# One more written-out order for an attention and feed-forward kernel on a single core

## The chip, the core and the metric

The kernel runs on one core of a Trainium2 chip. A core has a matrix engine (PE, with its weight loads shown apart as PEld), a vector engine (DVE), a scalar engine (ACT), a general engine (POOL) and a queue engine (SP) that mostly starts transfers. Each engine works through its own list of instructions strictly in the order in which the program gives them, and waits at semaphores for what the others produce. The metric is the device time of one execution in microseconds (us), lower is better.

## The reference

The input is attention with a forget gate (batch 8, heads 8, sequence 576, head width 64), followed by a bilinear feed-forward layer over the 4608 tokens. Cut to what is computed:

```python
scores = q @ k.T / sqrt(64)                      # per batch and head, 576 x 576
cum    = cumsum(log(clip(f, 1e-4, 1)))           # along the sequence
scores = where(causal, -1e9, scores + cum[:, None] - cum[None, :])
attn   = exp(scores - rowmax); attn = attn / (rowsum(attn) + 1e-9)
x      = (attn @ v), heads side by side          # 4608 tokens x 512
out    = ((x @ w_a) * (x @ w_b)) @ w_out         # 512 -> 1536 -> 512
```

## The kernel before

**Attention.** Work is cut into pairs of heads: t = 0 to 31, four pairs for each batch b = t // 4. Two pairs form a half batch u = 0 to 15. Queries are taken in blocks of 128 rows, i = 0 to 4 (block 4 has 64 rows), and the blocks are put into four groups g: (1, 0), (2), (3), (4). For each half batch and group PE computes scores (`qk_group`, L390). In the first two batches the decay is added by PE itself, by two small matmuls, and DVE takes the row maximum (`do_max`, L484); later DVE adds the decay and takes the maximum in one instruction (`do_decay`, L508). Then ACT does the exponential with its sum (`do_exp`, L537 and L543), DVE the reciprocal (`do_recip`, L552), and POOL scales the probabilities (`do_norm`, L560). The probabilities are turned by PE in batch 0 (`pe_tr`, L584, copied out by a cast) and by a DMA transpose from the SP queue from batch 1 on (`do_tr`, L576): part A0 holds query blocks 0 and 1, A1 block 2, B blocks 3 and 4. PE multiplies them with v (`do_pv` L604 to L616, `do_pv4` L629), and a cast brings the result into the array xT. Casts on ACT have line L137, those on DVE and POOL L141, scaled ones on POOL L139.

**Inputs.** q, k and v of a batch are loaded in fp32 by the SP queue (L264, L280), cast to fp16 (by POOL, in batch 0 by ACT or POOL) and q and k are turned by DVE (`transpose_qk`, L294). The prefix sum of the gate runs at the start, on ACT (logarithm, L208) and DVE (L205 to L223), in two column parts, 0 to 255 and 256 to 575.

**Feed-forward.** Tokens are taken in chunks starting at t0 = 0, 256, 512 (256 tokens each), 768 (384), six of 512 tokens and a last one of 384. For each chunk twelve pairs of matmul groups (psa and psb, `ff_mm`, L877, four matmuls each), a cast of psa by ACT or DVE (`ff_copy`), a product by DVE (`ff_mul`, L888), then the output matmuls (pso, `ff_out`, L897), a copy (`ff_ocopy`) and a store. A chunk can begin when the attention of its tokens is in xT. The chunks of early batches are interleaved with the attention of later ones.

**Filler.** Forty filler groups (`filler`, L174), each of four matmuls of 128 columns on the identity matrix, occupy PE where nothing else stands; their result is not used. They need the identity, which POOL makes (`constants`).

**What sets the order.** Every step is created as an `Op` with a number (its place of creation), one or more engines that may do it, and its dependencies. The list `ORDER` gives the sequence in which the 2342 steps are emitted, and so the order on each engine; the letters of `CHOICE` give the engine of each step that could go to more than one. Both are written out by hand in the file; nothing is planned when the kernel is built. Rings of buffers (four for the PSUM tag ff, two for the scores sc, three for loads n32, two for cast inputs n16) are handed out in the same sequence, and a step that reuses a buffer waits for the users of its previous content. The field `size` of an `Op` is read by nothing in this file.

Numbers that the text below needs: 0 is the identity, 61 the clearing of padding (POOL). 45 and 60 are ACT's two table loads, 47 and 53 the two logarithms. 65 and 69 turn the first halves of k and q of batch 0 (DVE); 67 and 68 cast that half of q, 75 and 76 the other half; 49 and 50 make the rows of columns 0 to 255 of the prefix sum, 55, 56 and 57 those of columns 256 to 575 (DVE). 91 and 116 are the first score groups (g = 0) of half batches 0 and 1, 141 the second (g = 1) of half batch 0. 363 and 364 are the score groups g = 0 and g = 1 of half batch 3 (pairs 6 and 7), 367 and 395 their row maxima for block 1, 373 and 401 those for block 0, 368 is the first exponential of pair 6, 379 its maximum for block 2. 446 and 443 turn q and k of batch 2. 1680 and 1685 are the two output copies of chunk 0 and 1681 the store of the first. 467 is the first score group of half batch 4, 471 its first decay step, 426 and 435 the value products of blocks 0 and 1 of pairs 6 and 7. 345, 346 and 347 are the DMA transposes A0, A1, B of pair 4; 354, 355, 356 those of pair 5; 423, 424, 425 of pair 6; 432, 433, 434 of pair 7.

Of the kernel before, what the change touches and what calls it, by code (L numbers as in the profile page):

```python
# [37 lines left out]
def kernel(  # L38
# [13 lines left out]
    B, H, S, D = q.shape  # L52
# [7 lines left out]
    TW = S // NSLOT // 2  # L60
# [236 lines left out]
    def batch_inputs(b):  # L297
# [4 lines left out]
        for which, part, gm in items:  # L302
# [18 lines left out]
            ld = op("S", "ldqk", lambda _, which=which, hh=hh: load_qk(b, which, hh))  # L321
# [13 lines left out]
            tp = op("D", "tqk", lambda _, which=which, hh=hh: transpose_qk(b, which, hh), cas)  # L335
# [633 lines left out]
    for n in [256, 256, 256, 384] + [512] * 6 + [384]:  # L969
# [13 lines left out]
        215 81 216 202 203 276 204 7 201 180 207 208 281 285 181-183 1641 90 1642 441 187 317 289 188 189  # L983
        318 290 166 323 324 295 297 296 190 1645 1643 1644 319 325 217 218 1646 1647 165 1648 88 229 192 231
        459 291 221 223 191 230 257 224 258 209 232 255 222 279 184 256 280 286 235-237 444 238 329 205 186
# [5 lines left out]
        1682-1684 1680 316 364 340 249 1685 283 251 443 379 252 376 20 250 1687 404 380 1688 1691 398 381  # L991
        449 344 407 546 1689 1690 409 452 382 408 1693 372 1692 1695-1697 365 1694 347 348 371 464 349 357
# [6 lines left out]
        523 483 1737 1740-1742 492 493 488 489 509 494 524 510 477 516 539 525 526 1738 527 470 451 462 497  # L999
        498 1743 495 466 428-430 499 431 547 484 437 439 438 440 490 530 531 500 457 491 537 501 1745 1746  # L1000
# [4 lines left out]
        553 551 606 636 566 573 1791 574 557 558 575 576 607-609 653 1790 1793 1794 1792 637 559 578 577 579  # L1005
        555 610 611 580 552 1795 1798 1799 650 615-617 582-584 581 1796 560 639 548 612 642 556 620 622 627
        654 600 544 614 618 1800 1803 1804 1807 621 585 613 587 619 629 623 624 586 626 1805 625 630 1801
        588-590 1806 591 593 592 628 1808 1811 657 1809 1813 1810 1812 669 1815 1817 702 703 739 704 651
        1816 643 1814 709 670 705 1819 1820 638 710 655 1818 711 1823 676 1821 1825 671 1822 640 712-714
# [119 lines left out]
```

## Time and profile before

| what | value |
|---|---|
| median of 3 runs | 405.43 us (403.7 to 407.23) |
| the profiled execution, whole | 402.69 us |
| its span, first to last instruction | 400.9 us |
| granted PE clock, mean | 0.985 of full |
| PE busy | 378.9 us (95%) |
| DVE, ACT, POOL busy | 315.5, 250.6, 262.8 us |
| transfers, mean | 201 GB/s |

The profiled execution took 1.8 us more than its span; that is what lies before the first and after the last instruction. A table by stretch of time gives the busy time of each engine in it, the granted PE clock as a share of full speed, and the busy share of the 16 DMA engines (above 1 where packets overlap). A row of the timeline begins with its start in us from the beginning of the span and its length; in square brackets stands how long the engine sat idle before it and what ended that idle time. SPq is the issuing of transfers by the SP queue.

### The profile page before, as it was taken

How to read it: one execution, taken by the hardware profiler on the slowest of the kernel's cores; microseconds unless marked ns; L12 is line 12 of the kernel's file. 1: busy time of each engine (PE TensorE's matmuls, PEld its weight loads, DVE VectorE, ACT ScalarE, POOL GpSimd, SP SyncE). 2: the span in 40 equal slices, each digit the busy share in tenths (PEclk: the TensorE clock that was granted, in tenths of full speed). 3: DMA queues.
4: the chain of work that ended last, by engine and by line, in shares of the span. 5: the costliest groups of instructions: out<-in, count | busy, mean ns of one | idle time of the engine just before them, and what ended most of it. 6: DMA issues, size and time to landing. Idle time of an engine off the chain costs nothing.

```text
span 400.9 us, 10798 instructions
## 1 busy us (share of the span) xinstructions
PE 378.9 (95%) x3856; PEld 209.3 (52%) x3856; DVE 315.5 (79%) x958; ACT 250.6 (63%) x756; POOL 262.8 (66%) x438
## 2 busy tenths in 40 slices
PE   5679799989999999999999999999999999999996
PEld 5557575765846544444545454544454444444553
DVE  5879997979998988989899789899959893373450
ACT  2678895768768777758785777675868673310111
POOL 4988899787967796979696948697858753000000
PEclk9869999999999999999999999999999999999999
DMA  7999999999999999999899998999997827101102
GB/s 245 261 217 224 253 284 224 233 209 225 208 281 224 267 199 305 202 310 191 270 217 286 238 301 168 242 242 243 255 199 192 151 68 177 54 0 53 55 2 78
DMA packets 149466, 80.71 MB, mean 201 GB/s; under 512 B 130660, under 2 KB 133476, under 8 KB 149412
## 3 DMA queue, kind: packets, MB, share of 16 engines
q1 hardware_dynamic: 145492, 75.02, 79.1%
q0 software_dynamic: 3696, 4.72, 7.0%
q8 instruction: 30, 0.49, 0.5%
q10 hardware_dynamic: 224, 0.28, 0.2%
q14 instruction: 24, 0.20, 0.1%
HBM read 52.20 MB, written 9.58 MB: 154 GB/s over the span
## 4 chain that ended last, share of the span: by engine, by line
PE 69%; DMA 8%; DVE 8%; POOL 5%; ACT 4%; issue 4%; SPq 0%; POOLq 0%; ACTq 0%; DVEq 0%
PE psb L877 20%; PE psa L877 20%; PE pso L897 16%; PE sc L390 7%; DVE st L484 3%; PE pv L604 2%; DMA PTB<-PB 2%; POOL PA L560 2%; DMA spread<-cum_d 2%; DMA k<-in_k_dram 2%; PE idle L174 1%; DVE ht L888 1%; DVE S L508 1%; DMA out_dram<-osb 1%; DMA xT<-PA 1%
## 5 line engine op out<-in xcount | busy, mean ns | idle before, releaser
L877 PE MATMUL psb<-xT,wb 128*128 128x512 f16 (+2 forms) x528 | 115.2, 341 | 2.4 <-DVE a L141 1.3
L877 PE MATMUL psa<-xT,wa 128*128 128x512 f16 (+2 forms) x528 | 115.2, 341 | 0.5 <-ACT osb L137 0.2
L508 DVE CUSTOM_DVE_ANT_0 S<-sc,spread 128x128 f32<-128x128 f32 (+3 forms) x192 | 104.3, 567 | 7.8 <-PE sc L390 6.7
L560 POOL TENSOR_SCALAR PA<-PA,st 128x128 f16<-128x128 f16 (+2 forms) x180 | 84.4, 482 | 33.8 <-DVE st L552 19.8
L897 PE MATMUL pso<-wout,ht 128*128 128x512 f16 (+1 forms) x444 | 98.4, 374 | 0.0
L888 DVE TENSOR_TENSOR ht<-psb,a 128x512 f16<-128x512 f32 (+2 forms) x132 | 76.7, 588 | 14.1 <-PE psb L877 10.1
L543 ACT ACTIVATE PA<-S,st 128x256 f16<-128x256 f32 (+2 forms) x144 | 71.9, 501 | 22.9 <-DVE st L508 21.4
L877 PEld LDWEIGHTS <-wb 128*128 128x128 f16 x528 | 49.8, 98 | 45.7 <-issue 6.8
L877 PEld LDWEIGHTS <-wa 128*128 128x128 f16 x528 | 50.4, 98 | 42.7 <-issue 2.0
L560 POOL TENSOR_SCALAR PB<-PB,st 128x512 f16<-128x512 f16 (+1 forms) x90 | 62.8, 712 | 10.6 <-DVE st L552 5.9
L897 PEld LDWEIGHTS <-ht 128*128 128x128 f16 x444 | 41.8, 98 | 48.1 <-issue 2.8
L137 ACT CAST a<-psa 128x512 f16<-128x512 f32 (+2 forms) x85 | 42.7, 511 | 34.8 <-PE psa L877 33.4
L390 PE MATMUL sc<-kT,qT 32*128 32x128 f16 (+5 forms) x960 | 41.3, 272 | 6.8 <-DVE qT L294 4.6
L543 ACT ACTIVATE PB<-S,st 128x512 f16<-128x512 f32 x48 | 34.3, 716 | 8.1 <-DVE st L508 7.4
L484 DVE TENSOR_REDUCE st<-sc 128x1 f32<-128x576 f32 (+8 forms) x48 | 31.4, 693 | 6.8 <-PE sc L390 5.2
L141 DVE CAST a<-psa 128x512 f16<-128x512 f32 (+2 forms) x47 | 26.2, 558 | 11.3 <-PE psa L877 10.8
L390 PEld LDWEIGHTS <-qT 32*128 32x128 f16 (+1 forms) x960 | 19.0, 96 | 28.8 <-issue 12.3
L552 DVE RECIPROCAL st<-st 128x2 f32<-128x2 f32 x128 | 18.6, 157 | 11.5 <-ACT PB L543 6.1
L537 ACT ACTIVATE PB<-S,st 128x576 f16<-128x576 f32 x24 | 18.6, 775 | 13.9 <-DVE st L508 5.0
L543 ACT ACTIVATION_READ_ACCUMULATOR PA<-S,st 128x1 f32 x144 | 27.2, 189 | 0.0
L137 ACT COPY osb<-pso 128x512 f32<-128x512 f32 (+1 forms) x26 | 14.4, 563 | 20.3 <-PE pso L897 18.6
L141 POOL CAST k<-k 128x1152 f16<-128x1152 f32 (+2 forms) x16 | 22.1, 1384 | 5.0 <-DMA k<-in_k_dram 5.0
(87 smaller groups left out, 449.8 us busy)
## 6 DMA issues: line engine op xcount, KB each, us to landing
spread<-cum_d SPq DMA_DIRECT2D x24, 576.0 KB, 5.9
out_dram<-osb SPq DMA_DIRECT2D x35, 256.0 KB, 4.0
k<-in_k_dram SPq DMA_DIRECT2D x15, 576.0 KB, 6.5
q<-in_q_dram SPq DMA_DIRECT2D x15, 576.0 KB, 6.9
v<-in_v_dram SPq DMA_DIRECT2D x32, 256.0 KB, 6.7
wout<-in_moe_w_out_dram POOLq DMA_DIRECT2D x3, 512.0 KB, 11.0
wa<-in_moe_w_a_dram POOLq DMA_DIRECT2D x1, 1024.0 KB, 13.9
v<-in_v_dram SPq DMA_DIRECT2D x8, 128.0 KB, 6.0
```

Source lines behind the costliest of these rows:

```text
L137: nc.scalar.copy(out=out_, in_=in_)
L141: ENG[e].tensor_copy(out=out_, in_=in_)
L390: nc.tensor.matmul(out=dst, lhsT=lhsT, rhs=rhs, start=start, stop=stop, skip_group_check=True)
L484: nc.vector.tensor_reduce(out=m if i == 4 else st[:, 2 * i:2 * i + 2][:, h:h + 1] if isinstance(x, list) else m, in_=y, axis=AXX, op=MAX, ...
L508: nc.vector.tensor_tensor_reduce(out=o, in0=x, in1=y, scale=-1.0, scalar=3e38, op0=ADD, op1=MIN, accum_out=m)
L537: nc.scalar.activation(out=p_blocks(t, 4), in_=T[("s" if direct else "z", t, 4)], func=EXP, bias=st[:, 8:9], scale=sign, accum_out=st[:, 1 ...
L543: nc.scalar.activation(out=p_blocks(t, i)[:, :, h, :], in_=x.rearrange("p (j k) -> p j k", k=128), func=EXP, scale=sign, bias=st[:, c:c + ...
L552: nc.vector.reciprocal(out=st[:, 20 + 2 * i:22 + 2 * i], in_=st[:, 10 + 2 * i:12 + 2 * i])
L560: ENG[e].tensor_scalar(out=p, in0=p, scalar1=st[:, c:c + 1], scalar2=1.0, op0=MUL, op1=MUL)
L877: nc.tensor.matmul(out=p[:, 0:n], lhsT=w16[:, db, 128 * fb:128 * fb + 128], rhs=xTflat[db][:, t0:t0 + n], start=(db == 0), stop=(db == 3))
L888: nc.vector.tensor_tensor(out=ht[:, 0:n], in0=T.pop(("psb", t0, fb))[:, 0:n], in1=T.pop(("a16", t0, fb))[:, 0:n], op=MUL)
L897: nc.tensor.matmul(out=o, lhsT=T[("ht", t0, fb)][:, 128 * tb:128 * tb + 128], rhs=wout16[:, fb, c], start=(fb == 0), stop=(fb == 11))
```

## The change

Two calls get the argument `size=TW` (TW is 9), and `ORDER` and `CHOICE` are replaced. The steps, their dependencies, the buffers and their counts are the same. In `CHOICE` 88 steps change engine, by kind:

| step | ACT to DVE | DVE to ACT | POOL to ACT |
|---|---|---|---|
| cast of psa, 256 / 384 / 512 columns | 6 / 3 / 14 | 8 / 3 / 7 | |
| output copy, 512 columns | 7 | 7 | |
| value results, 512 columns | 2 | 5 | |
| value results, 256 columns | 3 | 1 | |
| value results, 64 columns | 9 | 4 | |
| turned probabilities of batch 0 | 1 | 4 | |
| casts of q, batch 0 | | | 4 |

The order of PE is nearly the same: from its 497th of 567 steps on (chunk 3712) it is identical, and before that most steps move by up to a few places. Of the forty filler groups 23 instead of 17 stand ahead of the first score group, 6 instead of 13 between the first and the second, and two stand at places 190 and 250 of PE's list, where there were none beyond place 112.

```diff
-            ld = op("S", "ldqk", lambda _, which=which, hh=hh: load_qk(b, which, hh))
+            ld = op("S", "ldqk", lambda _, which=which, hh=hh: load_qk(b, which, hh), size=TW)
...
-            tp = op("D", "tqk", lambda _, which=which, hh=hh: transpose_qk(b, which, hh), cas)
+            tp = op("D", "tqk", lambda _, which=which, hh=hh: transpose_qk(b, which, hh), cas, TW)
...
     ORDER = """
-        42 44 43 61 0 1 59 46 52 62 63 45 47 48 15 35 64 66 49 67 26 3 68 31 53 54 38 10 22 2 70 65 25 14 50
-        71 72 74 9 51 69 55 11 73 60 33 23 18 29 91 34 104 30 105 78 12 106 92 110 27 267 84 75 85 112 76 77
-        107 41 93 86 36 19 5 98 111 113 94 32 56 100 8 13 99 28 6 95 79 114 116 117 119 123 118 124 115 101
-        57 125 141 129 135 97 126 109 108 120 130 136 225 131 148 103 96 102 122 128 226 137 121 127 211 212
...
-        1662 1664 322 293 336 337 1665 1666 545 333 354 1669 300 345 277 263 308 309 306 264 1667 1668 355
-        305 288 341 1671 265 266 282 346 342 1670 313 1673 1674 314 1677 442 1675 310 338 1672 1676 363 367
-        395 315 401 373 445 461 312 343 368 369 446 370 311 396 403 541 374 402 397 375 339 1678 1679
-        1682-1684 1680 316 364 340 249 1685 283 251 443 379 252 376 20 250 1687 404 380 1688 1691 398 381
-        449 344 407 546 1689 1690 409 452 382 408 1693 372 1692 1695-1697 365 1694 347 348 371 464 349 357
...
-        393 390 394 425 416 426 422 435 1718 436 467 471 1719 427 417 479 472 1721 478 504 418 1720 1723
...
+        0 1 8 40 32 42 44 59 31 18 3 9 33 30 36 43 6 13 62 63 2 64 46 22 52 45 47 53 60 66 12 48 5 24 10 70
+        54-57 19 67 68 65 71 28 72 38 74 78 49 14 50 84 69 73 75 76 37 51 91 267 61 29 92 104 93 94 23 77 58
+        34 105 15 85 16 98 106 95 4 99 110 111 270 107 100 86 112 116-118 79 96 101 97 123 124 109 113 129
+        135 82 108 119 120 103 125 126 136 141 102 211 114 41 115 130 122 225 131 137 128 121 226 127
...
+        255 300 293 294 332 302 1655 280 244 304 256 541 326 287 1657 1659 299 345 334 249 250 1656 305 307
...
+        288 310 263 264 282 341 313 1670 342 1673 1674 1677 314 327 338 363 446 1672 1675 315 1676 367 373
+        251 368 395 340 369 343 311 401 443 375 543 370 396-398 1678 252 402 283 1679 1682 463 1680 1683
+        1684 312 374 316 1685 403 364 379 1687 1689 1688 339 381 344 449 1691 1692 399 1695 452 407 380 409
...
+        390 434 467 393 394 448 1720 542 425 1718 471 479 478 1721 472 1722 504 473 512 465 456 511 480 474
...
     CHOICE = """
-        SAPDPPPPPAAPPPPPADADDDADADDAAADAAADADDAADDAAAADADAAADAAADAAAAAAAAAAAAADAAAAADAAAADDADDAADAADADAAAAA
...
+        SAPDPPPAAAAAAPPPDAADDADAADDDDADAAADADAAAADADAAAADAAAAADDAAAAAADAAAAAAADDAAADAADDAAAAAAAAAAADADADAAA
...
```

More of the change, by code (lines that the diff above doesn't have):

```diff
@@ new lines @@
+        531 532 1747 1749 1748 533 534 529 535 536 540 549 594 1750 561 1751-1754 1757 635 1758 458 562 595
[5 rows of a table added]
+        620 585 621 587 622 623 588 589 1798-1800 1803 1801 624 586 626 1805 657 669 670 625 590 702 591 671
+        672 592 593 640 1804 1807 1808 1811 629 1809 709 704 711 630 643 628 832 739 1806 645 677 679 710
+        703 1810 705 1813 655 1812 1815 712 706 1817 1814 1816 1819 676 1820 1818 1821 708 1823 644 707 638
+        678 673 713 680 1822 1824 681 662 715 675 641 1825 1827-1829 1826 658 665 659 1830 661 666 833
@@ new lines @@
+        746 785-788 783 1885 818 827 1886 1887 778 1890 764 789 819 825 855 1888 820 784 791 790 826 1889
+        821 822 900 902 817 823 824 828 1891-1893 838 841 867 1894 907 1895 901 1896 869 874 876 903 1897
+        875 877 909 937 1898 1899 836 1900 839 878 904 1901 905 1902 1904 1903 1906 1907 1910 879 868 870
+        860 856 1905 871 872 906 908 845 880 938 941 1908 873 1909 857 910 846 942 1030 859 858 863 864
+        881-883 911 1912 914 915 884 912 1911 1914 1915 1913 916 885 865 888 1027 917 889 921 918 890 886
[9 rows of a table added]
@@ new lines @@
+        2193 2189 2190 2196-2198 2201 2202 2194 1620 1621 2195 2199 1626 1627 2203 2206 2208 2204 1625 1619
+        1622 2207 2210 1628 2200 2211 2209 2205 2212-2218 2220 2219 2222 2223 2226 2224 2221 2228 2227 2225
+        2229-2231 2234 2232 2233 2236 2235 2237 2238 2240 2239 2241-2243 2246 2244 2245 2248 2247 2250-2253
+        2249 2254-2256 2259-2261 2264-2266 2262 2263 2269 2270 2257 2258 2267 2271 2274 2275 2272 2276 2277
+        2268 2273 2278-2291 2294 2292 2293 2295 2298 2296 2300 2297 2299 2302 2303 2301 2304 2306-2308 2305
@@ L1079 @@
+        2309-2311 2314 2312 2313 2316 2315 2318 2320 2319 2322 2321 2323 2317 2324 2327-2329 2332 2325 2326
+        2330 2331 2333 2334 2337-2341 2335 2336
     """
     CHOICE = """
[L1081 to L1083 removed]
+        SAPDPPPAAAAAAPPPDAADDADAADDDDADAAADADAAAADADAAAADAAAAADDAAAAAADAAAAAAADDAAADAADDAAAAAAAAAAADADADAAA
@@ L1084 @@
+        DADDADADDDDAADAAADDADADDDADAAADAAAAADADAAAAADAADAADDAAAAAADDADDAAAAADADAAAAAAADDAAAAAADADAAAADADAAD
+        AAADDDADAADDADADDDAAAAAADAAAAAADADDDAAAAAAADDAADDADAADADADDADDADAADADDAAAAAAS
     """
```

58 lines of the change are left out of this document (20 added, 38 removed), and 116 rows, old and new, of the table ORDER.

## The prediction

> **What bounds the kernel now.** I read the page's head first, then the table by stretch of time, then what PE waited for.
>
> ```profile
> span 400.9 us, 10798 instructions
> PE 378.9 (95%) x3856; PEld 209.3 (52%) x3856; DVE 315.5 (79%) x958; ACT 250.6 (63%) x756; POOL 262.8 (66%) x438
> ```
> ```profile
> 0.00:13.00 13.00, 5.83 (x68) 5.66 (x68) 7.75 (x20) 3.63 (x6) 6.67 (x18) 1.00 0.86 247
> 13.00:40.00 27.00, 22.89 (x412) 18.46 (x416) 23.09 (x58) 21.64 (x70) 23.86 (x39) 0.81 1.06 232
> 40.00:60.00 20.00, 17.23 (x324) 13.49 (x325) 18.65 (x43) 17.57 (x54) 17.69 (x28) 1.00 1.10 268
> 60.00:80.00 20.00, 18.79 (x288) 12.62 (x273) 16.71 (x39) 13.12 (x46) 17.18 (x26) 1.00 1.12 230
> 80.00:100.00 20.00, 17.98 (x264) 11.84 (x264) 16.97 (x67) 15.00 (x51) 16.22 (x30) 1.00 1.05 217
> 100.00:200.00 100.00, 99.53 (x982) 52.87 (x982) 89.42 (x303) 73.41 (x229) 80.01 (x132) 1.00 1.04 246
> 200.00:300.00 100.00, 99.47 (x901) 46.49 (x902) 87.31 (x293) 69.94 (x214) 75.37 (x124) 1.00 1.05 240
> 300.00:340.00 40.00, 40.00 (x310) 18.11 (x311) 30.89 (x99) 25.97 (x74) 25.81 (x48) 1.00 0.69 144
> 340.00:401.00 61.00, 57.15 (x340) 29.72 (x338) 24.75 (x41) 10.31 (x21) 0.00 (x0) 0.99 0.12 42
> ```
>
> Columns after the length are PE, PEld, DVE, ACT, POOL, clock, DMA share. The reader is to see two kernels in one. From 100 to 340 us PE idles 0.47 + 0.53 + 0 = 1.0 us: matmuls bound it, their number is fixed, and no order can win more than that 1.0. Before 100 us PE idles 7.2, 4.1, 2.8, 1.2 and 2.0 us, 17.3 in all, while DVE is busy 23.09 of 27 and 18.65 of 20: there the softmax chain sets the pace, and there alone a new order can earn something. The last 3.85 us of PE idleness (61 less 57.15) are the final copy and store, whose order does not change.
>
> ```profile
> PE sc L390 <- DVE qT L294: 4.6, 1, 4.6
> PE sc L390 <- DVE xT L223: 1.7, 1, 1.7
> PE pv L616 <- DMA xT<-PA: 1.5, 1, 1.5
> PE psb L877 <- DVE a L141: 1.3, 1, 1.3
> ```
>
> These are PE's longest waits whose cause lies in the order; each occurs once.
>
> **The change, part by part.** The sum is made against the profiled execution, 402.69 us (span 400.9 and 1.8 around it). The median of the runs is 405.43, 0.7% above it, so I carry the difference over to the median.
>
> *The size arguments* are read by nothing: 0.
>
> *The start, to 22 us.*
>
> ```profile
> 8.28 0.76 DVE L216 CAST wout<-cum_f 64x256 f16<-64x256 f32 x1
> 10.39 1.22 DVE L294 STREAM_TRANSPOSE kT<-k 128x576 f32<-128x576 f32 x1 [0.55 <-POOL k L141]
> 11.45 0.72 DVE L219 SCALAR_TENSOR_TENSOR xT<-wout,lsel,cum_f 64x256 f16<-64x256 f16 x1
> 12.09 1.19 DVE L294 STREAM_TRANSPOSE qT<-q 128x576 f32<-128x576 f32 x1
> ```
> ```profile
> 7.11 0.78 ACT L208 ACTIVATE cum_l<-cum_f 128x256 f32<-128x256 f32 x2 [4.28 <-DVE cum_f L205]
> 11.64 1.50 ACT L137 CAST k<-wout 128x640 f16<-128x640 f32 x2 [3.75 <-DVE kT L294]
> 13.16 1.28 ACT L201 ACT_TABLE_LOAD   x1
> ```
> ```profile
> 13.34 0.40 PE L390 MATMUL sc<-kT,qT 32*128 32x256 f16 x8 [4.64 <-DVE qT L294]
> 14.40 4.32 PE L174 MATMUL idle<-ident 128*128 128x128 f16 x52
> 18.65 0.50 PE L390 MATMUL sc<-kT,qT 32*128 32x256 f16 x8
> 19.29 0.32 PE L390 MATMUL sc<-kT,qT 32*128 32x384 f16 x1
> ```
>
> ACT now takes the casts of q: free at 7.9, table load 1.28 to about 9.3, two casts 1.50, done about 10.9, before DVE wants them. DVE turns k at 10.39 as before, because POOL's cast of k ends there. But between k and q now stand two small steps, 0.76 + 0.72, of which only the second stood there: 10.39 + 1.22 + 1.48 + 1.19 = 14.3. The first scores come at 14.3, not 13.34: +1.0. Against it the column part 256 to 575 of the prefix sum is finished before 10.4 us, so that the second score group of half batch 0 no longer waits 1.7 us for it. The other half of q is cast on ACT behind the turning of its first half (a ring of two buffers): 14.3 + 1.5 = 15.8, ahead of its turning on DVE (two maxima after 15.4, so about 16.9). The two effects cancel by my count when DVE reaches block 2 (+1.0 and −1.0). Bounds: the late start in full, +1.0, and the wait in full less what the late start eats, −1.0. I take 0.
>
> *The stretch from 62 to 72 us.*
>
> ```profile
> 63.86 1.29 DVE L484 TENSOR_REDUCE st<-sc 128x2 f32<-128x512 f32 x2 [0.74 <-PE sc L390]
> 65.86 1.20 DVE L294 STREAM_TRANSPOSE qT<-q 128x576 f32<-128x576 f32 x1
> 70.17 0.96 DVE L484 TENSOR_REDUCE st<-sc 128x2 f32<-128x768 f32 x1 [1.85 <-PE sc L390]
> ```
> ```profile
> 65.97 0.47 ACT L543 ACTIVATE PA<-sc,st 128x256 f16<-128x256 f32 x1 [2.98 <-DVE st L550]
> ```
> ```profile
> L141 DVE COPY osb<-pso 128x512 f32<-128x512 f32 x11 | 7.5, 686 | 5.6 <-PE pso L897 4.8 <-PE psa L877 0.6
> ```
>
> DVE idles 0.74 us for the scores of half batch 3, then 1.85 for the next group, because PE cannot overwrite the scores until ACT has made eight exponentials of up to 0.47 us each. In the new order the turning of q (446, 1.20 us) stands ahead of the first maximum and fills the 0.74. The two output copies 1680 and 1685 move from ACT to DVE and stand in the second hole: 2 x 0.69 = 1.37 of the 1.85. The maximum of block 0 of pair 6 (373) also comes third less late, so that the exponentials start about 1 us earlier. Gain 0.74 + 1.37 = 2.1 us of DVE time; bounds 0 (the holes only move) and 2.6 (both close).
>
> *The stretch from 82 to 88 us.*
>
> ```profile
> 84.57 0.53 PE L616 MATMUL pv<-xT,nv 128*64 128x128 f16 x12 [1.53 <-DMA xT<-PA]
> ```
> ```profile
> 86.07 0.42 DVE L508 CUSTOM_DVE_ANT_1 S<-sc,spread 128x256 f32<-128x256 f32 x1 [2.05 <-POOL PB L560]
> ```
>
> PE waits 1.53 us for a transposed block (pair 6) and only then makes the scores of half batch 4, which DVE awaits: its 2.05 us of idleness are the same stall (POOL had long been done). The new order puts the scores (467) ahead, and 426 eighteen places later. Gain 1.5, counted once; bounds 0 and 2.05.
>
> *Casts that change engine.*
>
> ```profile
> L137 ACT CAST a<-psa 128x512 f16<-128x512 f32 x52 | 29.6, 574 | 17.7 <-PE psa L877 16.5 <-DVE st L508 1.1
> L141 DVE CAST a<-psa 128x512 f16<-128x512 f32 x20 | 13.7, 686 | 3.7 <-PE psa L877 3.5
> ```
>
> Seven more casts of 512 columns go to DVE than leave it: 7 x 0.686 = 4.8 us, partly repaid by the other kinds in the table of the change: about +2.3 of DVE's 315.5 by counts and mean lengths. Most lies after 146 us, where DVE is idle 10 us in a hundred and PE sets the pace: hidden, and it costs up to 2.3 if that cover fails. By the lists about 1.1 us of added DVE work stands ahead of the products of chunk 512, in the stage where DVE counts: +1.1.
>
> *The SP queue.*
>
> ```profile
> 57.03 7.41 SPq L576 DMA_TRANSPOSE xT<-PA  x4
> 67.38 7.43 SPq L576 DMA_TRANSPOSE PTB<-PB  x2
> ```
> ```profile
> PTB<-PB SPq DMA_TRANSPOSE x28, 4.2
> xT<-PA SPq DMA_TRANSPOSE x8, 4.4
> ```
> ```profile
> 81.06 0.23 PE L616 MATMUL pv<-xT,nv 128*64 128x128 f16 x2
> ```
>
> Transposes are issued slowly here, 7.4 us for four and for two, and land 4.2 to 4.4 us later. Transpose 355 (A1 of pair 5) moves behind 347, 356 and the store 1681, which itself waits for copy 1680: 57.0, three transposes at 7.41 / 4 = 1.85 each, the loads between (64.4 to 67.4 now) 3, the two B parts 7.4, store and wait an estimated 2, its own 1.85: issued by 76.9, landed at 81.3. Its product ran at 81.06 (the last row) and would be wanted some 2 us earlier. Pair 7's A0 (432) also moves behind 424. I charge +0.6; bounds 0 and +3.
>
> *Two fillers in the full stage*: the 13 groups in the row of 52 took 4.32 us, 0.33 each, so +0.5 with a kind switch; bounds 0 and 0.7.
>
> Sum: 0 − 2.1 − 1.5 + 1.1 + 0.6 + 0.5 = **−1.4 us**: 401.3 for a profiled execution, **404.0** as a median. For stretches after 100 us I add nothing for new stalls; the old order had 1.0 us of them, so this can only cost, 0 to +3.
>
> **A rule against it.** PE's clock is granted at 0.81 on average from 13 to 40 us and 1.00 afterwards. After the idle 4.64 us the first score group takes 14.40 − 13.34 = 1.06 us, the second one 19.29 − 18.65 = 0.64: a cold group costs 0.42 more. In the new order the fillers can begin earlier (the identity is POOL's first work), six more groups precede, and the first scores come 1.0 later, so that PE's idle gap stays near 5 us or grows; between the two score groups stand 6 fillers where 13 stood. If PE stays cold through all eight score groups of batch 0, six more than now pay 0.42: +2.5 us, which is a rival below. [...] The 0.42 of the trace agrees with a slower clock after the gap.
>
> **The rivals.**
>
> 1. *Everything lands* (chance 0.20). Start −1.0, holes −2.6 and −2.05, casts and queue hidden, fillers 0.5: −5.1 at the end, some of it lost at the pinned transposes, say −4.5: 400.9. For it: PE has 17.3 us of idleness to give. Against: from 40 to 100 us POOL is 81 to 88% busy and the DMA share is over 1, so the next producer is close.
> 2. *The holes only move* (0.14). DVE is as loaded, and each gain meets the next late producer: 0 ± 0.5, 405.4. This is also the case of a change that does nothing.
> 3. *The SP queue takes over* (0.14, slower). PE works in order, so each us by which 355, 432 and the B parts of pairs 6 and 7 land after their place in PE's list is lost for good. The DMA share is 1.12 there, so issues wait for the queue. With three such places 1.6 us late each, 4.9 − 1.4 = +3.5: 408.9. It decides once transposes land more than 0.5 us late on average at the three places.
> 4. *PE stays cold* (0.10): −1.4 + 2.5 = +1.1, 406.5.
>
> **How the numbers follow.** My forecast has 0.42, 403.0 to 405.2. A difference of 1% (401.4 and 409.5) is about what a measurement of this kernel can tell from no change; the runs shown spread by 0.9%. Faster by over 1%: most of rival 1 and a little of the forecast, 0.23. Slower by over 1%: the upper part of rival 3, and new stalls in the full stage, 0.11. Within 1%: 0.66. The range 400.0 to 408.5 leaves about one in ten on either side.
>
> **What would show it.** In the profile after: no wait of PE for L223; first scores near 14.3; DVE's holes of 1.85 and 2.05 gone; PE idle from 40 to 100 us nearer 3.5 than 6.0; from 100 to 340 at most 1.5. The forecast is wrong if PE waits for transposes near 80 to 95 us by more than 2 us in all, if the clock from 13 to 40 falls well below 0.81, or if PE shows new waits for DVE's casts after 146 us.

## The result, and the profile after

The changed kernel takes 409.63 us as a median (407.03 to 414.62, 20 runs) against 404.99 (401.59 to 407.63, 20 runs) of the kernel before: ratio 1.0118, 95% interval 1.0092 to 1.0144. It is slower by about 4.8 us, outside the predicted range. The ratio leaves out runs in a slow state, such as the one of 414.62 us, and so is not exactly that of the medians. Its profiled execution took 410.75 us. That one lies 1.1 above its median, and the profiled one of before 2.3 below its own, so the two traces differ by 8.1 us (8.0 by their spans), more than the medians do.

The page's head of the changed kernel, and then its table by stretch of time (columns as before: PE, PEld, DVE, ACT, POOL, clock, DMA share, GB/s):

```profile
span 408.9 us, 10795 instructions
PE 384.0 (94%) x3856; PEld 211.1 (52%) x3856; DVE 317.5 (78%) x964; ACT 253.7 (62%) x754; POOL 258.2 (63%) x434
```
```profile
13.00:40.00 27.00, 19.41 (x327) 15.11 (x328) 20.65 (x50) 20.85 (x68) 22.41 (x42) 0.75 1.09 256
40.00:60.00 20.00, 17.97 (x351) 14.14 (x349) 18.84 (x45) 18.04 (x53) 16.88 (x27) 1.00 0.97 223
60.00:80.00 20.00, 18.11 (x281) 11.97 (x279) 16.76 (x39) 12.95 (x46) 17.55 (x29) 1.00 1.14 238
80.00:100.00 20.00, 19.24 (x271) 12.47 (x269) 18.07 (x70) 16.47 (x55) 17.26 (x30) 1.00 1.20 218
100.00:200.00 100.00, 99.69 (x970) 53.48 (x972) 88.66 (x303) 71.97 (x222) 77.16 (x126) 1.00 1.02 241
200.00:300.00 100.00, 99.53 (x879) 46.19 (x872) 89.02 (x293) 68.72 (x207) 78.33 (x129) 1.00 1.01 236
300.00:340.00 40.00, 37.06 (x329) 16.93 (x327) 31.71 (x105) 26.32 (x76) 21.90 (x43) 0.96 0.57 131
```

What PE waited for, the longest in total first (us in total, times, longest):

```profile
PE sc L390 <- DVE qT L294: 5.2, 1, 5.2
PE psP L584 <- POOL spread L560: 4.4, 3, 2.9
PE sc L390 <- DVE xT L141: 3.1, 3, 2.5
PE pv L629 <- DMA PTB<-PB: 1.9, 1, 1.9
```

The wait for L223 is gone, and so is the one of 1.5 for a transposed block. In their place stand 4.4 us for POOL's scalings (0.7 before), 1.9 for a transpose, and one that had no counterpart at all: 3.1 us for DVE's copies, 2.5 of it at once. The stretch from 300 to 340 us, which PE filled completely before, now has 2.94 us of idleness and a clock of 0.96.

A table of when PE reaches the same step shows where the distance arises. It gives the start in the kernel before and, for the other kernels (the last four are experiments, below), the difference to it, all read from PE's timeline of one execution each:

| PE step | before | changed | decay step first | early list only | late list only | scores first |
|---|---|---|---|---|---|---|
| first group of chunk 0 | 33.89 | +1.77 | +1.06 | +1.70 | +0.57 | −0.22 |
| scores g = 0, half batch 3 | 62.83 | +2.86 | +2.20 | +2.17 | +0.55 | −0.22 |
| first group of chunk 256 | 70.94 | +0.87 | +0.21 | +0.17 | +0.55 | −0.23 |
| scores g = 3, half batch 3 | 79.34 | +3.10 | +3.12 | +0.62 | +1.35 | −0.16 |
| scores g = 0, half batch 4 | 85.03 | +0.86 | +0.88 | −1.63 | +1.30 | −2.17 |
| first group of chunk 512 | 97.66 | +1.08 | +1.11 | −1.40 | +1.29 | +0.06 |
| first group of chunk 768 | 118.21 | +2.07 | +2.13 | −0.69 | +2.75 | +0.06 |
| first group of chunk 2688 | 265.50 | +3.92 | +4.00 | −0.59 | +4.60 | |
| first group of chunk 3200 | 304.61 | +8.16 | +3.34 | −0.61 | +3.94 | |
| first group of chunk 4224 | 373.59 | +8.05 | +3.24 | −0.61 | +3.83 | |

The early list of before can itself stand 1.3 us apart at chunk 512 from one execution to the next ("late list only" has that list up to there, and stands at +1.29), so single differences below that are not read; jumps inside a column are. Of the 8.05 us, 1.08 are there at chunk 512, 2.84 are added by chunk 2688, and 4.24 in one place just before chunk 3200. Here is that place, on DVE and then on PE:

```profile
302.09 0.29 DVE L508 CUSTOM_DVE_ANT_0 S<-sc,spread 128x128 f32<-128x128 f32 x1 [4.04 <-PE sc L629]
...
303.34 0.17 DVE L552 RECIPROCAL st<-st 128x2 f32<-128x2 f32 x1 [0.95 <-ACT PA L543]
303.42 1.19 DVE L294 STREAM_TRANSPOSE kT<-k 128x576 f32<-128x576 f32 x1
...
304.48 1.19 DVE L294 STREAM_TRANSPOSE qT<-q 128x576 f32<-128x576 f32 x1
305.52 0.20 DVE L141 CAST xT<-sc 128x64 f16<-128x64 f32 x1
```
```profile
295.56 6.22 PE L897 MATMUL pso<-wout,ht 128*128 128x512 f16 x28
301.70 0.35 PE L629 MATMUL sc<-PTB,nv 128*64 128x64 f16 x10
...
305.78 0.23 PE L390 MATMUL sc<-kT,qT 32*128 32x128 f16 x2 [2.47 <-DVE xT L141]
306.48 0.50 PE L390 MATMUL sc<-kT,qT 32*128 32x128 f16 x14 [0.47 <-DVE xT L141]
306.91 4.43 PE L897 MATMUL pso<-wout,ht 128*128 128x512 f16 x12
```

DVE sits 4.04 us ahead of a decay step (pair 28, block 0, head 0; number 1468), and what it waits for is PE's `pv4` of pair 26 (L629, number 1450). The decay step needs nothing of that result. But `pv4` of a pair writes its 64 columns into spare columns of the score tile of the pair two further on (`T["spare"]`, columns 448 to 511 of its first half), and in the new list 1450 is written two places ahead of 1468. PE does 28 output matmuls (6.22 us) before it comes to `pv4`. Then DVE has two turns of 1.19 us to do before the copy at 305.52 that frees the score tile, and PE's next score group waits 2.47 and 0.47 us. The twelve output matmuls behind it take 4.43 us, against 2.76 in the kernel before:

```profile
300.42 2.76 PE L897 MATMUL pso<-wout,ht 128*128 128x512 f16 x12
```

The instruction lists show the wait itself. The same instruction, in the changed kernel and in the one of the first experiment:

```
changed:          L508 ISA S,st<-sc_5809,spread_79 128x128 [waits PE_49]
decay step first: L508 ISA S,st<-sc_5809,spread_79 128x128
```

In the list of before all 44 decay steps of this kind (block 0, two heads, 22 pairs) stand ahead of the `pv4` that shares their tile; in the new list 40 do. Of the other three, one shows a wait too:

```profile
174.05 0.29 DVE L508 CUSTOM_DVE_ANT_0 S<-sc,spread 128x128 f32<-128x128 f32 x1 [1.12 <-PE sc L629]
```

### The profile page after: what moved, and what is told of

Its sections match the earlier page's. It is cut to its first block, busy times and chain, and to the rows that moved or that the text cites. A ratio compares the mean times of both kernels' runs of the same rounds, so it can differ in the third digit from the quotient of the medians.

```text
span 408.9 us, 10795 instructions
## 1 busy us (share of the span) xinstructions
PE 384.0 (94%) x3856; PEld 211.1 (52%) x3856; DVE 317.5 (78%) x964; ACT 253.7 (62%) x754; POOL 258.2 (63%) x434
## 4 chain that ended last, share of the span: by engine, by line
PE 77%; DVE 10%; DMA 5%; POOL 3%; ACT 2%; issue 2%; SPq 0%; DVEq 0%; POOLq 0%; ACTq 0%
PE psb L877 21%; PE psa L877 21%; PE pso L897 20%; PE sc L390 7%; DVE S L508 3%; PE pv L604 2%; DMA q<-in_q_dram 2%; DVE st L484 2%; DMA cum_f<-in_f_dram 1%; DMA PTB<-PB 1%; DVE kT L294 1%; PE pv L606 1%; PE sc L629 1%; DVE qT L294 1%; ACT PA L543 1%
## 5 line engine op out<-in xcount | busy, mean ns | idle before, releaser
L560 POOL TENSOR_SCALAR PA<-PA,st 128x256 f16<-128x256 f16 (+2 forms) x180 | 83.8, 479 | 42.1 <-DVE st L552 27.8
L897 PE MATMUL pso<-wout,ht 128*128 128x512 f16 (+1 forms) x444 | 100.0, 378 | 0.0
L137 ACT CAST a<-psa 128x512 f16<-128x512 f32 (+2 forms) x80 | 40.3, 506 | 54.4 <-PE psa L877 52.2
L390 PE MATMUL sc<-kT,qT 32*128 32x128 f16 (+5 forms) x960 | 42.2, 272 | 10.4 <-DVE qT L294 5.2
L141 DVE CAST a<-psa 128x512 f16<-128x512 f32 (+2 forms) x52 | 30.3, 582 | 6.0 <-PE psa L877 5.3
L458 POOL TENSOR_SCALAR_AFFINE_SELECT spread<-spread 128x768 f32<-128x768 f32 x24 | 20.8, 868 | 9.7 <-DMA spread<-cum_d 9.7
```

Of the source, the lines that this page charges most:

```text
L137: nc.scalar.copy(out=out_, in_=in_)
L141: ENG[e].tensor_copy(out=out_, in_=in_)
L390: nc.tensor.matmul(out=dst, lhsT=lhsT, rhs=rhs, start=start, stop=stop, skip_group_check=True)
L458: nc.gpsimd.affine_select(out=c[:, :, 0:SM].rearrange("p h (j k) -> p h j k", k=128), in_=c[:, :, SM:2 * SM].rearrange("p h (j k) -> p h j ...
L560: ENG[e].tensor_scalar(out=p, in0=p, scalar1=st[:, c:c + 1], scalar2=1.0, op0=MUL, op1=MUL)
L897: nc.tensor.matmul(out=o, lhsT=T[("ht", t0, fb)][:, 128 * tb:128 * tb + 128], rhs=wout16[:, fb, c], start=(fb == 0), stop=(fb == 11))
```

## Experiments

Each ratio is to the kernel before as it ran beside that experiment. Its medians there were 403.17 to 404.63 us, so times from different experiments are compared by their ratios.

**One number moved two places.**

```diff
-  1461 1469 1462 1504 1430 1450 1463 1468 2121 1451
+  1461 1469 1462 1504 1430 1468 1450 1463 2121 1451
```

> The changed kernel with one number of the list moved two places: the decay step 1468 (pair 28, block 0, head 0, DVE) is written ahead of pv4 of pair 26 (1450, PE) and not behind it; each engine's own sequence is the same as in the changed kernel. Theory (a step that is written behind pv4 waits for it, since pv4 writes spare columns of the same score tile): DVE's idle 4.04 us at 302 goes, PE's waits of 2.5 and 0.5 us at 304 to 306 go, the granted clock of 300 to 340 is 1.00 again, time 4 to 5 us less than the changed kernel: 404.6 to 405.6. Rival (DVE's own sequence, two turns of 1.2 us ahead of the two copies that free the score tile, holds PE in any case): 0 to 1.5 us less, 408.1 to 409.6. Rival (the loss is spread over many places and the one place is an accident of the profiled run): nothing, 409.6.

Measured: 405.05 us, ratio to before 1.0027 (1.0001 to 1.0052); the changed kernel had 1.0118. DVE's idle time at this step is gone, and PE fills the stretch again (DVE's timeline, then the table by stretches):

```profile
298.05 0.28 DVE L508 CUSTOM_DVE_ANT_0 S<-sc,spread 128x128 f32<-128x128 f32 x1
...
299.64 0.17 DVE L552 RECIPROCAL st<-st 128x2 f32<-128x2 f32 x1 [1.30 <-ACT PA L543]
299.72 1.21 DVE L294 STREAM_TRANSPOSE kT<-k 128x576 f32<-128x576 f32 x1
...
300.80 1.20 DVE L294 STREAM_TRANSPOSE qT<-q 128x576 f32<-128x576 f32 x1
302.16 0.22 DVE L141 CAST xT<-sc 128x64 f16<-128x64 f32 x1 [0.17 <-PE sc L629]
```
```profile
300.00:340.00 40.00, 40.00 (x352) 18.61 (x351) 32.33 (x105) 27.19 (x77) 24.86 (x47) 1.00 0.66 150
```

The theory held: by the ratios 0.91% of 405, 3.7 us, are this one place, slightly less than the 4 to 5 expected, and in the trace 4.8 (+8.16 against +3.34). The two turns stand ahead of the copy here too, and cost nothing, because they now begin 3.7 us earlier.

**The same in the kernel before.**

```diff
-  1504 1468 1498 2128 1464 1465 1467 1470 2129 1450 1451
+  1504 2128 1464 2129 1450 1468 1498 1465 1467 1470 1451
```

> The kernel before with the same decay step (1468) written behind pv4 of pair 26 (1450) and not ahead of it; four steps that need it or follow it on their engines are written behind it too, and each engine's own sequence is that of the kernel before. Theory (written place): DVE shows a new idle time of 3 to 4 us ahead of this step near 298 us, waiting for PE; behind it stand only one turn (1.2 us) and not two ahead of the copy, so PE loses 0.7 to 1.5 us: 405.7 to 406.5 against 405.0. Rival (only the engines' own sequences matter): no new idle time and no difference.

Measured: 408.08 us, ratio 1.0094 (1.0064 to 1.0123). DVE's timeline has the wait, nearly to the hundredth:

```profile
300.23 0.29 DVE L508 CUSTOM_DVE_ANT_0 S<-sc,spread 128x128 f32<-128x128 f32 x1 [4.02 <-PE sc L629]
...
302.70 1.22 DVE L294 STREAM_TRANSPOSE qT<-q 128x576 f32<-128x576 f32 x1 [2.04 <-POOL q L139]
```

The mechanism is shown from both sides. Its price was underrated: 0.7 to 1.5 us were expected and the ratio says about 3.8; the trace shows 2.5 at this place (+1.60 at chunk 2688, +4.05 at chunk 3200), and where the rest lies stays open. The wait of 2.04 us for POOL's cast of q is not new. It stands in the kernel before as well:

```profile
298.63 1.24 DVE L294 STREAM_TRANSPOSE qT<-q 128x576 f32<-128x576 f32 x1 [2.04 <-POOL q L139]
```

That cast stands on POOL behind a scaling whose reciprocal stands on DVE behind the decay step, so the whole chain of reciprocal, scaling, cast, turn and copy moves back with it: the turn begins at 302.70 and not 298.63, where the kernel as a whole runs 1.6 us late.

**POOL's cast moved behind the scalings.** In the new list the cast of the last 64 rows of v (83) stands ahead of the scalings of pair 3, and POOL waits there for the load; in the kernel before it came after five scalings, four of them of pair 3, and found its data there:

```profile
25.53 1.39 POOL L139 TENSOR_SCALAR q<-q 128x1152 f16<-128x1152 f32 x1
29.07 0.60 POOL L141 CAST nv<-v 64x512 f16<-64x512 f32 x1 [2.15 <-DMA v<-in_v_dram]
29.65 0.82 POOL L560 TENSOR_SCALAR spread<-spread,st 128x256 f16<-128x256 f16 x2
```
```profile
28.76 0.83 POOL L560 TENSOR_SCALAR spread<-spread,st 128x256 f16<-128x256 f16 x2
29.56 0.60 POOL L141 CAST nv<-v 64x512 f16<-64x512 f32 x1
```
```diff
-  271 83 154 155 150 273 151 156 134 161 157 80 140 167 233 162 163 146 139 275 153 21 133 253
+  271 154 155 150 273 151 156 134 161 157 80 140 167 233 162 163 146 139 153 21 133 83 275 253
```

> The changed kernel with POOL's cast of the last 64 rows of v of batch 0 (step 83) moved from ahead of the scalings of pair 3 to behind four of them (134, 140, 139, 133; 146 and 153 too), and the load that reuses its buffer (275) with it. Theory (POOL stands 2.15 us at this cast for its load, which lands near 29 us in both kernels, and everything behind it is late): POOL's idle 2.15 goes, PE's wait of 2.9 for turned probabilities goes, the first feed-forward group starts near 33.5 instead of 35.66, and 1 to 2.2 us of it is left at the end: 407.4 to 408.6. Rival (the 2 us are made up between 65 and 88 us in any case, where the loss fell from 2.9 to 0.9): 0 to 0.5 us less, 409.1 to 409.6.

Measured: 409.01 us, ratio 1.0108 (1.0072 to 1.0144). The wait is gone and chunk 0 begins at 33.37 and not 35.66, 2.3 us earlier. Of these, 0.4 are left at chunk 512. So the rival was right: at the score group g = 3 of half batch 3 both kernels are late again (+2.70 and +3.10), and the reason is in PE's waits of this kernel:

```profile
PE pv L629 <- DMA PTB<-PB: 1.8, 1, 1.8
...
PE psP L584 <- POOL spread L560: 0.9, 2, 0.5
```

The wait of 1.8 us is not the whole of it. Behind it PE's granted clock is 0.50 for 3.4 us (77.07 to 80.49), so PE does about 1.7 us less work in them (half of 3.4; a feed-forward group of four matmuls of 256 columns takes up to 1.06 us there and 0.60 behind it); in the changed kernel the clock there is 1.00.

**Both edits.**

> Both edits together. Theory (two separate causes that make up nearly the whole difference): the gains add, 5 to 7 us less than the changed kernel, 402.6 to 404.6, so level with the kernel before or up to 2 us below it. Rival (the start's loss is made up anyway): 4 to 5 less, 404.6 to 405.6. Rival (neither is the cause): 408.5 to 409.6.

Measured: 404.57 us, ratio 1.0009 (0.9979 to 1.0038): the first edit's gain and at most a little more. In its trace the load that the second edit moves was late itself, and POOL stood for it instead:

```profile
40.65 1.39 POOL L141 CAST k<-k 128x1152 f16<-128x1152 f32 x1 [5.10 <-DMA k<-in_k_dram]
```

**The two lists joined at chunk 512.** What remained was divided by taking one list up to the start of chunk 512 and the other from there, in both ways, with 1468 ahead of 1450.

```diff
-  ORDER = the changed list
+  ORDER = the first 700 steps of before, then the rest as the changed list has it     (late list only)
+  ORDER = the first 660 steps of the changed list, then the rest as before has it     (early list only)
```

> The list of the kernel before for its first 700 steps (to just past the start of chunk 512, about 100 us), then the list of the changed kernel for the rest, with the decay step 1468 ahead of pv4 of pair 26 as in the first experiment. Theory (what is left of the loss with that step mended lies in the full stage: PE changes more often between attention and feed-forward matmuls, 0.1 to 0.3 us each, and does two fillers): like the kernel before at 98 us, 2 to 2.5 us later at 304, and so 2 to 2.5 us slower than before: 405.4 to 405.9 if before is at 403.4. Rival (what is left comes from the start and the early stage): at most 0.7 us slower than before, up to 404.1.

> The mirror of it: the list of the changed kernel for its first 660 steps (to just past the start of chunk 512), then that of the kernel before. Theory: the profiled offset at 98 us, about +1.1, is carried to the end and nothing is added, 404.0 to 404.9 if before is at 403.4; no idle time of 4 us on DVE near 300 us. Rival (early stage alone makes what is left, and the later list adds nothing): 405.0 and more. Rival (the gains between 62 and 88 us outweigh the start): 402.0 to 403.0.

Measured: late list only 405.54 us, ratio 1.0044 (1.0015 to 1.0074); early list only 402.52 us, ratio 0.9958 (0.9923 to 0.9992). The late list costs 1.8 us, slightly less than the 2 to 2.5 that the theory had. The early list does not cost; by itself it is faster than the kernel before by 1.7 us (0.3 to 3.1), which only the last rival allowed for. The same early list stands at −1.40 us at chunk 512 in this kernel and at +1.08 and +1.11 in the two others of the table. The table shows where they part: up to chunk 256 this kernel and the one with the decay step mended are level (+0.17 and +0.21), and 2.5 us apart at the score group g = 3 of half batch 3 (+0.62 and +3.12). There the second waits 2.56 us for the turned block B of pair 5 and this one does not wait. It was taken once more with the cast of v moved as above:

> The mirror hybrid (list of the changed kernel to the start of chunk 512, then that of before), with POOL's cast of the last rows of v (83) and the load behind it (275) moved behind the scalings, as in the second experiment. Theory (the early list gains 1.7 us by itself, and the cast's wait still costs some 0.5 of it): 1.5 to 2.7 us faster than before, ratio 0.993 to 0.996. Rival (the early list's gain was chance): ratio 0.998 to 1.002.

Measured: 402.72 us, ratio 0.9972 (0.9939 to 1.0004). In its trace it is 2.26 us ahead of the kernel before at chunk 256 and 1.94 behind at the score group g = 3: a wait of 2.4 us for block B, and a clock of 0.50 for 3.4 us behind it. The two results lie within each other's intervals; together they suggest that the early list is a gain of some 1 to 2 us, and the cast adds nothing to it that can be told. The first of the two is the one version here that beats both kernels beyond its interval. It does so by little, and among eleven versions one such result can be chance.

The late list's cost hardly shows as idle time (100 to 300 us: 0.78 us now, 1.0 before). It shows as longer steps. From the starts of PE's steps between 97 and 300 us, the time from one step to the next, by what comes next, with the counts in the list of before and in the changed one:

```
feed-forward group of 512, next is feed-forward        0.863 us
feed-forward group of 512, next is attention           0.959 us   (any size: 38 -> 43 such changes)
pv4, next is the value product / another pv4           0.16 / 0.18 us   (13 -> 7 / 7 -> 7)
pv4, next is feed-forward / a score group              0.28 / 0.48 us   (1 -> 4 / 0 -> 2)
filler group                                           0.23 and 0.32 us (0 -> 2)
```

That makes 5 x 0.096 = 0.5, then 0.85 for `pv4` (7 x 0.16 + 4 x 0.28 + 2 x 0.48 against 13 x 0.16 + 0.28, the pairs of `pv4` being as many as before), then 0.55 for the fillers: 1.9 us, of 2.2 that the trace with the decay step mended adds between chunk 512 and chunk 3200. This is a count, not an experiment, and it does not carry over whole to the kernel with the late list only. That kernel has no filler behind the start of chunk 256, and yet its trace adds 2.65 us between the same two chunks. In their place PE has a wait there that neither whole list has, ahead of a `pv4` at 107 us:

```profile
PE sc L629 <- POOL nv L141: 0.8, 1, 0.8
```

**The stretch from 62 us to chunk 512 alone.**

```diff
-  ORDER = the list of before
+  ORDER = the first 377 steps of before, the changed list up to its step 660, then the rest as before has it
```

> The list of the kernel before for its first 377 steps (to about 62 us), then that of the changed kernel to just past the start of chunk 512 (step 660 of its list), then that of the kernel before. So the two stretches that were to gain, 62 to 72 and 82 to 88 us, alone. Theory (the filled idle times of DVE and the moved score group are a gain by themselves): the start of chunk 512 comes 1 to 2.5 us earlier than in the kernel before, and the time is 1 to 2.5 us less, 400.9 to 402.4 if before is at 403.4. Rival (the changed kernel only made up there for its late start, and transposes and casts hold this stretch when it begins on time): within 0.5 us of before, 402.9 to 403.9.

Measured: 407.18 us, ratio 1.0091 (1.0057 to 1.0125). The joint itself did harm: the load of the decay row of pair 10 (541) came behind the transposes, and POOL stood for it with the scalings of pairs 4 and 5 in its queue:

```profile
POOL spread L464 <- DMA spread<-cum_d: 5.7, 1, 5.7
```

So it was repeated with that load ahead of the transposes (541 ahead of 354):

> The hybrid of the stretch from 62 us to the start of chunk 512, with the load of the decay row of pair 10 (541) issued ahead of the transposes of pairs 4 and 5, as in the changed kernel, so that POOL does not stand 5.7 us at the step that reads it (that stand came from the seam of the two lists). Theory (the filled idle times of DVE and the moved score group are a gain by themselves): start of chunk 512 1 to 2.5 us earlier than in the kernel before, ratio 0.994 to 0.998. Rival (the changed list only makes up there for a late start): ratio 0.999 to 1.002. In both cases POOL's idle time of 5.7 us near 65 us is gone and the time is some 3 us below that of the hybrid with the late load.

Measured: 405.40 us, ratio 1.0036 (1.0008 to 1.0064). The long wait of POOL was gone, and with it 0.55%, 2.2 us (3 were expected). There is no gain, and it is not clearly level either. In its trace PE loses 3.9 us between the score groups g = 2 and g = 3 of half batch 3, by a wait of 2.3 us for the turned block B of pair 5 and a clock of 0.50 for 3.4 us behind it (80.67 to 84.09), and wins 2.2 back by the next score group. The early list without its own beginning is worth nothing here; whether this joint does harm of its own was not tried.

**The first exponential of pair 6 ahead of a maximum.**

```diff
-  395 315 401 373 445 461 312 343 368 369
+  395 315 401 368 373 445 461 312 343 369
```

> The kernel before with one number of the list moved: the first exponential of pair 6 (368, ACT) is written ahead of the maximum of block 0 of pair 6 (373, DVE), which reads the same score tile; each engine's own sequence stays. Theory (two steps on one score tile wait for each other in the written order, even where both only read): the exponential starts 1.0 to 1.4 us earlier (64.6 to 65.0 and not 65.97), the maximum now waits for it and does not start earlier than it did; the next score group of half batch 3 comes 0.5 to 1.2 us earlier than 69.0; at the end 0 to 1 us less than before, 402.4 to 403.4. Rival (only a write and a read wait for each other): the exponential's start does not move.

```profile
65.47 0.47 ACT L543 ACTIVATE PA<-sc,st 128x256 f16<-128x256 f32 x1 [1.60 <-DVE st L484]
...
66.79 0.47 ACT L543 ACTIVATE PA<-sc,st 128x256 f16<-128x256 f32 x1 [0.76 <-DVE st L484]
...
67.94 0.47 ACT L543 ACTIVATE PA<-sc,st 128x256 f16<-128x256 f32 x1 [0.58 <-DMA xT<-PA]
```

The kernel runs 0.89 us late there as a whole, so the exponential starts at 64.58 by the times of before, 1.39 earlier: steps on one score tile wait for each other here in the written order even where both only read it. The two steps share one more tile, that of the maxima (st), into which both write. The kernel before shows that this is not the reason. In its half batch 1 each head has a score tile of its own:

```profile
19.57 0.95 DVE L484 TENSOR_REDUCE st<-sc 128x1 f32<-128x256 f32 x3 [0.65 <-PE sc L390]
20.96 0.29 DVE L484 TENSOR_REDUCE st<-sc 128x1 f32<-128x128 f32 x1 [0.43 <-ACT spread L543]
```
```profile
20.36 0.47 ACT L543 ACTIVATE spread<-sc,st 128x256 f16<-128x256 f32 x1 [0.94 <-DVE st L484]
```

Both heads' maxima of block 0 of pair 2 are written behind that exponential, which is of head 1. The one of head 0, the last of the three, is done at 20.52 while the exponential still runs; the one of head 1, on the exponential's score tile, waits for it.

The score group behind the moved exponential, which waits for the last of eight, does not come earlier (+1.06 against +0.89): the second exponential still stands behind the maximum and waits 0.76 us for it, and the third waits 0.58 for a transpose. Measured: 402.88 us, ratio 0.9976 (0.9944 to 1.0008): no gain that can be told from none.

**The score group of half batch 4 ahead of the value products**, in the kernel before:

```diff
-  425 416 426 422 435 1718 436 467 471 1719 427 417
+  425 416 467 422 435 1718 436 471 1719 426 427 417
```

> The kernel before with the first score group of half batch 4 (467, PE) written ahead of the value products of pairs 6 and 7 (426, 435), and 426 one feed-forward group later, so that PE has 467, 435 and 1719 (0.5, 0.2 and 0.44 us) to do while the transposed block of pair 6 is on its way; DVE, ACT, POOL and SP keep their sequences. Theory (the stall at 84 us, 1.53 us of PE and 2.05 us of DVE, is one stall and goes with the order): PE's wait there falls from 1.53 to at most 0.5, DVE's idle time ahead of its first decay step (2.05) falls by 1.5 or more, chunk 512 starts 0.8 to 1.5 us earlier against the score group g = 3 of half batch 3, and 0.8 to 1.5 us is left at the end: ratio 0.996 to 0.998. Rival (another late step takes the place of the stall): ratio 0.999 to 1.001.

Measured: 404.44 us against 403.17, ratio 1.0018 (0.9990 to 1.0046). PE's timeline and the table by stretches, of this kernel and then of before:

```profile
83.35 0.51 PE L390 MATMUL sc<-kT,qT 32*128 32x128 f16 x22 [0.27 <-ACT PB L537]
...
91.79 0.68 PE L390 MATMUL sc<-kT,qT 32*64 32x512 f16 x14 [0.99 <-DVE st L508]
```
```profile
80.00:90.00 10.00, 9.73 (x157) 6.99 (x151) 8.22 (x36) 6.35 (x24) 9.23 (x14) 1.00 1.12 192
90.00:100.00 10.00, 8.69 (x107) 4.77 (x104) 8.93 (x30) 8.40 (x27) 6.76 (x15) 1.00 1.02 242
```
```profile
80.00:90.00 10.00, 8.30 (x151) 6.49 (x151) 7.40 (x34) 6.71 (x25) 8.29 (x13) 1.00 1.12 209
90.00:100.00 10.00, 9.68 (x115) 5.36 (x113) 9.57 (x34) 8.29 (x28) 7.93 (x18) 1.00 0.99 225
```

The stall goes, exactly: the score group starts 2.17 us earlier and PE wins 1.43 us between 80 and 90. Between 90 and 100 it loses 0.99 of that again, now waiting for DVE's decay steps, and chunk 512 begins where it did (+0.06). The rival was right.

## Why the prediction was wrong

The step that failed is one sentence: "For stretches after 100 us I add nothing for new stalls; the old order had 1.0 us of them, so this can only cost, 0 to +3". The direction of the bound was right, its height and the value taken in it were not. After chunk 512 the trace lost 7.0 us, 4.2 to 4.8 at the decay step and 2.2 in longer steps; the ratios say 3.7 and 1.8. The argument went by each engine's own list and by the data that a step needs. It had no place for a wait that comes from the order *between* engines on one tile, though the two lists showed it. Nor had it a place for the second loss: it held that from 100 to 340 us the matmuls' "number is fixed", and took their time to be fixed with it. By the ratios the early list (−1.7), the late list (+1.8) and the decay step (+3.7) add up to +3.8 of the measured +4.8, within what intervals of about 1.2 us each leave open.

Point by point:

- *The size arguments*: the runs give no sign of an effect; none was looked for.
- *The start.* First scores predicted at 14.3, measured 14.35; the wait for L223 gone, as predicted. The net was not 0: the trace has +1.77 at chunk 0 and +2.86 at 62 us. The missing term is the cast of v that waits 2.15 us for its load. Taking that wait away moved chunk 0 by 2.3 us and the end by no more than the measurement can tell, since block B of pair 5 and the clock took it back, so it decided nothing.
- *62 to 72 us.* Predicted −2.1. In the changed kernel the distance falls from +2.86 to +0.87, −2.0, and it does so in every kernel with the whole early list (by 1.3 and 0.3 in the two that have only the stretch from 62 us). Right in size, but kept only in part, since the transposes follow.
- *82 to 88 us.* Predicted −1.5, bounds 0 and 2.05; measured −2.2 (+3.10 to +0.86). As a single edit it gave 0 at the end: the stall is one stall, as argued, but DVE's decay steps are next in line less than 1 us behind.
- *The SP queue.* Charged +0.6, bounds 0 and +3; the distance grows by 1.9 between the score groups g = 2 (+1.22) and g = 3 of half batch 3. The place was nearly right and the block wrong: not 355 (block A1 of pair 5) but 356 (block B), whose product PE now reaches at 76.9 and not 80.9. The rows are of the changed kernel and of the one with the decay step mended:

```profile
78.82 0.35 PE L629 MATMUL pv<-PTB,nv 128*64 128x64 f16 x10 [1.89 <-DMA PTB<-PB]
```
```profile
78.84 0.35 PE L629 MATMUL pv<-PTB,nv 128*64 128x64 f16 x10 [2.56 <-DMA PTB<-PB]
```

  The two come there 0.7 us apart and leave together: a landing sets the time. With the early list only, the block landed at 76.15 and there was no wait. So the third rival was right in kind and found one place, not three.
- *Casts that change engine.* +1.1 ahead of chunk 512 was too much; from the score group of half batch 4 to chunk 512 the distance grows by 0.2. Later they are hidden, as said: PE's waits for such casts after 146 us stay under 0.4 us each, apart from the place at 304. There the sign "new waits for DVE's casts after 146 us" is met, but the casts are late because DVE stood for `pv4`.
- *Fillers.* +0.5 predicted, 0.23 + 0.32 = 0.55 measured.

The terms up to chunk 512 add up to −1.9 in the prediction, and the early list alone measures −1.7 (−3.1 to −0.3). That agreement is partly luck: the start was too good by 2 to 3 us, the casts too dear by 0.9, and the transposes too cheap by 1.3. In the changed kernel's own trace chunk 512 comes 1.08 us later and not 1.9 earlier. Of the signs named, DVE's two holes are gone (its longest wait from 58 to 100 us is 1.0); PE idle from 40 to 100 us was to fall from 6.0 towards 3.5 and is 4.7; from 100 to 340 it was to be at most 1.5 and is 3.7. The clock from 13 to 40 us fell from 0.81 to 0.75, as the fourth rival feared; what that cost by itself was not tried.

What stays open: how much of the 1.8 us of the late list is its changes between kinds of matmuls, which were counted but not varied; and when block B of pair 5 lands. PE gets past it at 76.2 us in the two kernels with the early list only, and at 77.0, 78.2, 78.8 and 78.8 in the four with both new lists, one execution each.

## What to carry to other kernels

Where an order over several engines is written out, list the pairs of steps on different engines that touch the same tile, and see whether any pair changes sides: here one such pair, with each engine's own sequence and every data dependence the same, made a wait of 4.04 us, and its price was what stood ahead of the other step on its engine, 6.22 us of output matmuls. An engine that is 99.5% busy can still get slower without any new idle time: here the same steps took longer in another order (1.9 us by a count, not varied). A stall that an edit removes in a stage with several late producers is worth only the distance to the next of them (here 1.43 us of PE were won and 0.99 lost again within 10 us); before the place is priced, look for the next landing of a transfer and the next step of each engine behind it. A wait of PE of some 2 us can cost nearly as much again in a lower clock behind it: in three of these traces a clock of 0.50 for 3.4 us, some 1.7 us of work, followed waits of 1.83, 2.36 and 2.31 us for block B of pair 5; behind one of 2.56 us the clock stayed at 1.00.

## What the runs showed of the hardware

Two steps on one score tile keep to the written order here, by semaphores that stand in the instructions: in the changed kernel the decay step at 302.09 waited 4.04 us for `pv4`. They do so also when both read (in the kernel before, the maximum at 20.96 waited 0.43 us for the exponential at 20.36), and also when they touch different halves: in the changed kernel the decay step of head 1 at 174.05 reads the second 512 columns of its tile while `pv4` writes the first, and waited 1.12 us.

PE's granted clock fell behind short gaps. Behind the idle times of 2.47 and 0.47 us, with only two small matmuls between them, twelve matmuls of 512 columns took 4.43 us and not 2.76: 1.67 us more, a third of the 4.8 that this place cost in the trace; the clock was 0.50 from 306.91 to 310.32. In this trace it is 1.00 or 0.50 and changes at 13.37, 20.19, 30.43, 37.26, 306.91 and 310.32 us, each a multiple of 3.413 us from the others (296.95 us from the first to the last, 87 of them). The table takes stretches between such points, from the traces at hand:

| kernel | stretch, us | longest idle time of PE ahead of a step | PE busy in the stretch | clock in the next 3.4 us |
|---|---|---|---|---|
| changed | 303.50 to 306.91 | 2.47 | 0.66 | 0.50 |
| early list, cast moved | 73.61 to 77.02 | 2.36 | 1.05 | 0.50 |
| stretch from 62 us, load ahead | 77.26 to 80.67 | 2.31 | 1.10 | 0.50 |
| changed, cast moved | 73.66 to 77.07 | 1.83 | 1.57 | 0.50 |
| before, decay step last | 302.60 to 306.01 | 1.83 | 1.97 | 1.00 |
| decay step first | 74.21 to 77.63 | 2.56 | 2.07 | 1.00 |

In the last row the idle time of 2.56 us runs on into the next stretch, in which PE is busy for 2.20 us. The longest gap by itself does not tell the two kinds apart (1.83 us stands in both); the busy time of one such stretch does, in these six: 1.57 us and less in the one kind, 1.97 and 2.07 in the other. It does not settle the clock alone. In the first 40 us, with their many small matmuls, the clock fell behind stretches with 1.62 us of work (before, 20.47 to 23.88) and 1.53 (changed, 27.02 to 30.43), but it also stayed at 0.50 behind stretches with 2.62 (before, 23.88 to 27.29) and 2.43 (changed, 13.37 to 16.78). None of this was varied by itself.
